# Query powers from a matmul on the decay table, a first loop period in its own order, a table cleared in steps

## The chip, the cores and the metric

The kernel runs on one core of a Trainium2 chip. The metric is the device time of one execution in microseconds (us), and less is better. TensorE (PE in the profile, PEld for its weight loads), VectorE (DVE), ScalarE (ACT), GpSimd (POOL) and SyncE (SP) each run their own instruction queue in order. DMA transfers are issued from SP, ACT and POOL; an engine whose next instruction has to wait holds up all that stands behind it in its queue.

## The reference

Two layers follow each other. The first is a causal linear attention with a decay per head, for 4 sequences of 768 positions, 8 heads of 64 channels, worked in blocks of positions:

```python
Dmask = np.where(rel >= 0, lam ** rel, 0.0)              # decay inside a block
lam_pow = lam ** (pos + 1)                               # query powers
intra = (q k^T * Dmask) v
inter = (q * lam_pow) @ kv_state
out = intra + inter
kv_state = lam ** block * kv_state + (k * lam ** (block - 1 - pos))^T v
```

The second is a mixture of experts on the 3072 tokens of 512 channels that come out: logits with a bias by modality, the best of 8 experts per token, `relu(x @ w1[e]) @ w2[e]`, scaled by the softmax weight of the chosen expert.

## The kernel before

All arithmetic that matters is float32 or its split into two parts. A sequence is cut into 6 blocks of 128 positions, and two blocks make a half, loaded by one `load_half` into a tile `load` of which there are three (`LOADS`). The attention runs over 12 periods of a pair of blocks. The first pair is written out ahead of the loop, the others are turns `j` of `for j in range(1, pairs)`. In a period TensorE makes the scores of both blocks (`scores`, L235), the part of the output that comes from the carried state (`from_state`, L281), the part from inside the block (`outputs`, L288), the token rows and gate logits of the pair before (`tokens`, L299), and the key-value products for the next states (`key_values`, L255). VectorE multiplies the scores by the decay table (`masked`, L242), the keys by their decay (`keys`, L213), the queries by their powers (`queries`, L225), and adds a faded state to a key-value product (`carried`, L270). GpSimd multiplies the old state by the decay of a block (L268). The tile `qd` of scaled queries has one buffer, so the queries of a pair can be scaled only when `from_state` of the pair before has read its own.

The tables are made on the chip. `spread_decays` spreads the 8 decays to all partitions with a tiny matmul and lets VectorE run one scan for each of the 8 heads, which gives `dk`, 128 columns for a head (L85). Four more scans give the query powers `pq` (L91), after two copies that arrange the decays by pair of heads (L89).

The mixture part needs a table `inv` in DRAM that maps slots to tokens. It is first filled with a padding value by four transfers (`clear_table`, L177), and then each block's tokens are scattered into it by an indirect DMA that GpSimd issues (`write_slots`, L392). A sequence's six scatters are spread over the period after its routing is known; the first sequence's begin in turn 5 of the loop. Each scatter writes to a place known only at run time, so it waits for all four clearing transfers.

The order on an engine is fixed in three ways: `pinned` chains the instructions of an engine in the order in which they are written; `behind(a, b)` adds an edge, a real wait or, with `wait=False`, an order alone; and what is left free is placed by a planner that goes by its own estimate of when things are ready. The fades are pinned on GpSimd, the scatters are not: they are held behind the fades written before them and behind the matmul named in the code. SP's queue is the order of the loads: in turn `j` it issues half `3 + j`, when its buffer is free, and the four clearing transfers stand behind half 5, in turn 2.

After the attention, tiles of 256 tokens of one expert go through the two layers of that expert, with weights fetched for each tile.

Of the kernel before, what the change touches and what calls it, by code (L numbers as in the profile page):

```python
# [6 lines left out]
F32 = mybir.dt.float32  # L7
# [4 lines left out]
ALU = mybir.AluOpType  # L12
# [28 lines left out]
def linear_attention_moe(tc, qkv, lam, modality, wg, mbias, w1, w2, out):  # L41
    nc = tc.nc
    with ExitStack() as ctx:
# [32 lines left out]
        lamp = const.tile([P, NP], F32, name="lamp")  # L76

        def spread_decays():

            lp = ps.tile([P, 2, NP], F32, name="x", bufs=1)  # L80
            pinned(nc.tensor.matmul(lp.rearrange("p h a -> p (h a)"), row, lam1, start=True, stop=True))
            pinned(nc.vector.tensor_copy(out=lamb, in_=lp))
            for hl in range(2):
                for p in range(NP):
                    pinned(nc.vector.tensor_tensor_scan(  # L85
                        out=dk[:, hl, p, :], data0=lamb[:, hl, p : p + 1].to_broadcast([P, P]),
                        data1=anti, initial=0.0, op0=ALU.mult, op1=ALU.add))
            for hl, r in enumerate(halves2):
                pinned(nc.vector.tensor_copy(out=lamp[r], in_=lamb[r, hl]))  # L89
            for p in range(NP):  # L90
                powers.append(pinned(nc.vector.tensor_tensor_scan(  # L91
                    out=pq[:, p, :], data0=lamp[:, p : p + 1].to_broadcast([P, P]),
                    data1=zero, initial=1.0, op0=ALU.mult, op1=ALU.add)))

        def load_tile():

# [11 lines left out]
        zero = const.tile([P, P], F32, name="zero")  # L108
        nc.vector.memset(zero, 0.0)
        anti = const.tile([P, P], F32, name="anti")  # L110
        nc.gpsimd.affine_select(out=anti, in_=zero, pattern=[[1, P]], compare_op=ALU.not_equal,
                                fill=1.0, base=1 - P, channel_multiplier=1)
        dk = const.tile([P, 2, NP, P], F32, name="dk")
        pq = const.tile([P, NP, P], F32, name="pq")
        powers = []
        ident = const.tile([P, P], F32, name="ident")
        make_identity(nc, ident)

        wgt = const.tile([P, HB, NP, E], F32, name="wgt")

        def later(op):

            behind(op, powers[-1])
            return op


        iw = const.tile([P, HB, NP, P + E], F32, name="iw")
# [20 lines left out]
                                          in_=ident[r, r].unsqueeze(1).to_broadcast([D, NP, D]))  # L148

        def routing_constants():  # L150
            nc.vector.memset(onesb, 1.0)
            later(nc.gpsimd.affine_select(out=lowb, in_=onesb, pattern=[[1, P]], compare_op=ALU.is_gt,
                                          fill=0.0, base=0, channel_multiplier=-1))
            later(nc.gpsimd.iota(desc, pattern=[[-1, E]], base=E, channel_multiplier=0,
                                 allow_small_or_imprecise_dtypes=True))
            later(nc.gpsimd.memset(pay, 0))
            nc.gpsimd.iota(pay[:, :, 0:1], pattern=[[P, B * NC]], base=0, channel_multiplier=1)

            for m in range(2):
# [12 lines left out]
        def clear_table(ld):  # L172
            for i in range(2):
                part = inv[i * half_inv : (i + 1) * half_inv, :].rearrange("(p r) c -> p r c", p=P)
                for r in range(0, half_inv // P, some):
                    dst = part[:, r : min(r + some, half_inv // P)]
                    behind(nc.sync.dma_start(out=dst, in_=pad[:, : dst.shape[1]]), ld, wait=False)  # L177

        state = [const.tile([P, NP, D], F32, name=f"state{i}") for i in range(3)]
        kdec = const.tile([P, HB, NP, 2], F32, name="kdec")  # L180
# [4 lines left out]
        def load_half(g):  # L185
            t = load_tile()
            whole = slice(0, HB)
            for part in (slice(0, 2), slice(2, 4)) if g < LOADS else (slice(0, 4),):
                for c in (slice(i, i + 1) for i in range(HB)) if g == 1 else (whole,):
                    ld = nc.sync.dma_start(out=t[:, part, c], in_=source(g)[:, part, c])  # L190
                    if g == 1 and part.start == c.start == 0:
                        nc.sync.dma_start(out=wgt, in_=wg)
            loads.append(ld)
            return t

# [42 lines left out]
        def masked(g, sp):  # L238

            pt = work.tile([P, 2, NP, P], F32, name="pt", bufs=2)  # L240
            for hl in (slice(0, 1), slice(1, 2)) if g == 0 else (slice(0, 2),):
                pinned(nc.vector.tensor_tensor(out=pt[:, hl], in0=sp[:, hl], in1=dk[:, hl], op=ALU.mult))  # L242
            return pt

        def key_values(gs):
# [29 lines left out]
        def from_state(j, op, qd):  # L275

            c = HB * j % NC
            for p in range(NP):
                for blk in range(0 if c else 1, HB):
# [570 lines left out]
                halves[j] = load_half(j)  # L850

        identities()
        c0, c1 = slice(0, 1), slice(1, 2)
        list_constants()
        keep_busy(4)
        spread_decays()
        keep_busy(8)
        sps = [scores(0)]
        keep_busy(2)
        sps.append(scores(1))  # L860
        keep_busy(4)
        for blk in range(HB):
            pinned(nc.scalar.copy(out=kdec[:, blk], in_=dk[:, :, :, P - 1].rearrange("p h a -> p a h")))
        more(1)
        more(2)
        for to, src in ((mod, modality), (mb, mbias.partition_broadcast(P))):
            behind(nc.sync.dma_start(out=to, in_=src), loads[-1], wait=False)
        pts = [masked(0, sps[0])]
        kds[0] = keys(0, c0)
        pts.append(masked(1, sps[1]))  # L870
        qds[0] = queries(0, c1, eng=nc.gpsimd)
        op = outputs_begin()
        kp, _ = key_values([0])
# [1 line left out]
        xts[0], _ = outputs(0, pts[0], op)  # L875
        from_state(0, op, qds.pop(0))
        xts[1], _ = outputs(1, pts[1], op)
        keys(0, c1, kds[0])
        kp, _ = key_values([1])
        carried(1, kp)  # L880
        pinned(nc.scalar.copy(out=iw[:, :, :, P:], in_=wgt))
        more(LOADS)
        for j in range(1, pairs):
            turns = turned(j - 1)
# [2 lines left out]
            if routed is not None:  # L887
                rk = ranks(*routed)
            if j == 1:
                qds[1] = queries(1, c0)  # L890
                pts = [masked(gs[0], sps[0])]
                kds[1] = keys(1, c0)
                pts.append(masked(gs[1], sps[1]))
                queries(1, c1, qds[1])
                next(turns)
                next(turns)
                kp, _ = key_values(gs[:1])
                carried(gs[0], kp)
                keys(1, c1, kds[1])
# [7 lines left out]
            if j == pairs - 1:  # L907
                halved = [pinned(nc.scalar.copy(out=w1h[i], in_=raw1[i])) for i in range(2)]
            op = outputs_begin()
            from_state(j, op, qds.pop(j))  # L910
            if j > 1:
                mm = next(turns)
            if j == early + 1:
                write_slot(mm)
# [21 lines left out]
            if j > 1:  # L936
                next(turns)
# [96 lines left out]
        kept = [dk[:, t].rearrange("p a t -> p (a t)") for t in range(2)]  # L1034

        def run_early(n):

# [102 lines left out]
```

## Time and profile before

| | |
|---|---|
| median of 3 runs | 413.11 us (413.05 to 416.46) |
| the profiled execution | 412.88 us, span 411.2 us |
| granted TensorE clock, mean | 0.992 |
| PE busy | 395.3 us, 96% |
| DVE busy | 252.4 us, 61% |
| ACT busy | 181.6 us, 44% |
| POOL busy | 113.6 us, 28% |
| moved by DMA | 63.28 MB |

The span runs from the first to the last instruction of the core; the time of the execution has 1.7 us more around it. All times in the rows below are microseconds from the start of the span. "PE busy" says that TensorE has something in flight, not that it runs at its peak.

### The profile page before, as it was taken

The numbers are of one execution on the slowest core, as the hardware profiler recorded it, in microseconds if no ns is written. First come the engines' busy times: TensorE is split into PE (matmuls) and PEld (weight loads), VectorE is DVE, ScalarE is ACT, GpSimd is POOL, SyncE is SP. The second block draws the span as 40 slices with busy tenths as digits, with TensorE's granted clock in tenths as the row PEclk, the third lists the DMA queues.
The fourth block names the chain that finished last, engine by engine and source line by source line (L and its number), as shares of the span: only waits on it lengthen the run. The fifth ranks groups of instructions, "written<-read, shape, count | busy, mean of one in ns | idle before, by whom it ended". The sixth has DMA issues, their size and how long they took to land.

```text
span 411.2 us, 9569 instructions
## 1 busy us (share of the span) xinstructions
PE 395.3 (96%) x3839; PEld 354.5 (86%) x3840; DVE 252.4 (61%) x438; ACT 181.6 (44%) x274; POOL 113.6 (28%) x119
## 2 busy tenths in 40 slices
PE   8899999999999999999999999999999999999990
PEld 4799999888998987898989898998989899998970
DVE  8776886967989813583665738374664828374510
ACT  1233233225655514473654638273555637264510
POOL 6301143352376510321130402222030312202000
PEclk9999999999999999999999999999999999999996
DMA  7999999994910292211063676211020211100000
GB/s 288 392 363 373 389 348 348 338 390 133 330 41 30 51 396 106 64 40 68 1 213 125 233 255 220 92 30 58 22 80 27 56 51 47 51 2 28 27 29 20
DMA packets 22677, 63.28 MB, mean 154 GB/s; under 512 B 6751, under 2 KB 7263, under 8 KB 20578
## 3 DMA queue, kind: packets, MB, share of 16 engines
q1 hardware_dynamic: 14400, 42.83, 29.1%
q0 software_dynamic: 4768, 13.08, 9.6%
q10 hardware_dynamic: 3458, 6.69, 4.3%
q8 instruction: 32, 0.52, 0.5%
q14 instruction: 19, 0.16, 0.1%
HBM read 90.87 MB, written 14.07 MB: 255 GB/s over the span
## 4 chain that ended last, share of the span: by engine, by line
PE 61%; issue 21%; DMA 7%; POOL 5%; DVE 3%; another core or an unknown queue 1%; ACT 1%; POOLq 1%; DVEq 0%; ACTq 0%
DMA out_dram<-y,idx 7%; PE s L639 6%; PE s L642 6%; PE s L643 6%; PE o L288 5%; PE o L639 5%; PE o L643 5%; PE o L642 5%; PE x L299 5%; PE s L235 5%; PE o L281 3%; POOL out_dram L715 3%; PE kv L255 2%; POOL xg L591 2%; PE s L674 1%
## 5 line engine op out<-in xcount | busy, mean ns | idle before, releaser
L639 PE MATMUL s<-xh,w1h 128*128 128x256 f32 x384 | 108.9, 284 | 0.8 <-DVE hl L657 0.8
L642 PE MATMUL s<-xl,w1h 128*128 128x256 f32 x384 | 108.4, 282 | 0.0
L643 PE MATMUL s<-xh,w1l 128*128 128x256 f32 x384 | 107.9, 281 | 0.0
L657 DVE SCALAR_TENSOR_TENSOR hl<-s,hh 128x512 fp32r<-128x512 f32 x48 | 33.1, 690 | 83.9 <-ACT hh L656 83.2
L639 PE MATMUL o<-w2h,hh 128*128 128x512 f32 x192 | 75.9, 395 | 0.0
L643 PE MATMUL o<-w2h,hl 128*128 128x512 f32 x192 | 74.8, 390 | 0.0
L642 PE MATMUL o<-w2l,hh 128*128 128x512 f32 x192 | 74.8, 389 | 0.0
L639 PEld LDWEIGHTS s<-xh,w1h 128*128 128x128 f32 x384 | 72.0, 187 | 1.9 <-DVE hl L657 1.0
L643 PEld LDWEIGHTS s<-xh,w1l 128*128 128x128 f32 x384 | 72.8, 190 | 0.0
L642 PEld LDWEIGHTS s<-xl,w1h 128*128 128x128 f32 x384 | 72.2, 188 | 0.4
L556 DVE TENSOR_TENSOR w2l<-raw,w2h 128x1024 fp32r<-128x1024 f32 x48 | 58.8, 1225 | 11.0 <-ACT w2h L555 10.5
L656 ACT ACTIVATE hh<-s 128x512 fp32r<-128x512 f32 x48 | 28.7, 598 | 71.0 <-PE s L643 67.3
L556 DVE TENSOR_TENSOR w1l<-raw,w1h 128x1024 fp32r<-128x1024 f32 x46 | 53.5, 1217 | 4.9 <-ACT yn L703 3.4
L555 ACT CAST w2h<-raw 128x1024 fp32r<-128x1024 f32 x48 | 49.9, 1040 | 0.0
L591 POOL DMA_INDIRECT xg<-xs,idx x20 | 24.0, 1202 | 87.0 <-PE kv L626 82.8
L715 POOL DMA_INDIRECT out_dram<-y,idx x18 | 26.2, 1457 | 78.1 <-ACT y L731 74.7
L555 ACT CAST w1h<-raw 128x1024 fp32r<-128x1024 f32 x46 | 45.2, 1063 | 0.4 <-issue 0.4
L643 PEld LDWEIGHTS o<-w2h,hl 128*128 128x128 f32 x192 | 36.0, 188 | 7.6
L642 PEld LDWEIGHTS o<-w2l,hh 128*128 128x128 f32 x192 | 36.1, 188 | 7.1
L639 PEld LDWEIGHTS o<-w2h,hh 128*128 128x128 f32 x192 | 36.1, 188 | 7.1
L301 ACT COPY xn<-x 128x272 f32<-128x272 f32 x42 | 16.3, 388 | 46.1 <-PE x L299 43.0
L392 POOL DMA_INDIRECT inv<-pay,sloti x24 | 28.5, 1189 | 22.3 <-PE x L299 8.1
(215 smaller groups left out, 468.3 us busy)
## 6 DMA issues: line engine op xcount, KB each, us to landing
raw<-in_w_dram SPq DMA_DIRECT2D x52, 1024.0 KB
load<-in_qkv_dram SPq DMA_DIRECT2D x9, 2048.0 KB
xs<-xn ACTq DMA_DIRECT2D x24, 272.0 KB
load<-in_qkv_dram SPq DMA_DIRECT2D x8, 512.0 KB
load<-in_qkv_dram SPq DMA_DIRECT2D x2, 1024.0 KB
w2f<-in_w_dram SPq DMA_DIRECT2D x2, 1024.0 KB
w1h<-in_w_dram SPq DMA_DIRECT2D x2, 1024.0 KB
inv<-pad SPq DMA_DIRECT2D x2, 196.0 KB
```

Source lines behind the costliest of these rows:

```text
L235: pinned(nc.tensor.matmul(sp[:, hl, p, :], kt[r, p, :], qt[r, p, :], start=True, stop=True))
L288: mm = pinned(nc.tensor.matmul(op[blk][halves2[hl ^ blk], p, :], vt[:, (2 * p + hl) * D : (2 * p + hl + 1) * D], pt[:, hl, p, :], start=(g ...
L392: sc = nc.gpsimd.indirect_dma_start(out=inv, out_offset=bass.IndirectOffsetOnAxis(ap=at, axis=0), in_=pay[:, c, :], in_offset=None)
L555: cp = nc.scalar.copy(out=hi, in_=src)
L556: df = nc.vector.tensor_tensor(out=lo, in0=src, in1=hi.bitcast(F32), op=ALU.subtract)
L591: last = nc.gpsimd.indirect_dma_start(out=(to or xg)[t][:m], out_offset=None, in_=xs[:rows, :], in_offset=bass.IndirectOffsetOnAxis(ap=idx ...
L639: mm = pinned(nc.tensor.matmul(out, ah, bh, start=first, stop=False))
L642: pinned(nc.tensor.matmul(out, ah, bl, start=False, stop=False))
L643: return pinned(nc.tensor.matmul(out, al, bh, start=False, stop=last))
L656: act = nc.scalar.activation(out=hh[i], in_=hp, func=AF.Relu)
L657: low = nc.vector.scalar_tensor_tensor(out=hl[i], in0=hp, scalar=0.0, in1=hh[i].bitcast(F32), op0=ALU.max, op1=ALU.subtract)
L715: sc = nc.gpsimd.indirect_dma_start(out=out, out_offset=bass.IndirectOffsetOnAxis(ap=idx[:, t, 0:1], axis=0), in_=y, in_offset=None, bound ...
```

## The change

- `dk` gets 129 columns for a head instead of 128 (so do `zero` and `anti`), so that its last row holds the powers 1 to 128 of the decay. The two copies and four scans on VectorE that made `pq` are gone. `spread_powers` multiplies a selector `last` (only its last row is one) with columns 1 to 128 of `dk`, two matmuls into one PSUM tile, and ScalarE copies that tile to `pq`. The masks read `dk` in rows of 129.
- Ahead of the loop, the fillers `keep_busy(2)` and `keep_busy(4)` go; `spread_powers` stands between the scores of block 0 and block 1; the copies to `kdec` come before it. The second keys of the first half come earlier on VectorE. The first half of the next pair's queries goes to GpSimd.
- In turn 1 the state of the first block is used ahead of the first token group, and the second block's after its own state is made; the token groups stand between other work.
- `clear_table` is a generator: one clearing transfer in turn 2, one in turn 3, two in turn 4, each behind the load issued just before it.
- `wgt`, `mod` and `mb`, three small inputs, are loaded from GpSimd's queue instead of SP's. The routing constants that GpSimd makes (`lowb`, `desc`, `pay`, `pad`), and the loads of `mod` and `mb`, are ordered behind the second fade and no longer behind the last scan.
- Half 2 comes in three pieces, keys by rows first, values last; half 3 comes in two.

```diff
-            for hl, r in enumerate(halves2):
-                pinned(nc.vector.tensor_copy(out=lamp[r], in_=lamb[r, hl]))
-            for p in range(NP):
-                powers.append(pinned(nc.vector.tensor_tensor_scan(
-                    out=pq[:, p, :], data0=lamp[:, p : p + 1].to_broadcast([P, P]),
-                    data1=zero, initial=1.0, op0=ALU.mult, op1=ALU.add)))
+        def spread_powers():
+            pp = ps.tile([P, NP, P], F32, name="x", bufs=1)
+            for hl, r in enumerate(halves2):
+                pinned(nc.tensor.matmul(pp[r], last, dk[:, hl, :, 1:], start=True, stop=True))
+            pinned(nc.scalar.copy(out=pq, in_=pp))
...
-        dk = const.tile([P, 2, NP, P], F32, name="dk")
+        dk = const.tile([P, 2, NP, P + 1], F32, name="dk")
...
+        last = const.tile([P, D], F32, name="last")
+        nc.gpsimd.affine_select(out=last, in_=zero[:, :D], pattern=[[0, D]], compare_op=ALU.not_equal,
+                                fill=1.0, base=1 - P, channel_multiplier=1)
...
+        nc.gpsimd.dma_start(out=wgt, in_=wg)
         def later(op):
-            behind(op, powers[-1])
+            behind(op, fades[1], wait=False)
...
         def routing_constants():
+            for to, src in ((mod, modality), (mb, mbias.partition_broadcast(P))):
+                later(nc.gpsimd.dma_start(out=to, in_=src))
...
-                    behind(nc.sync.dma_start(out=dst, in_=pad[:, : dst.shape[1]]), ld, wait=False)
+                    yield behind(nc.sync.dma_start(out=dst, in_=pad[:, : dst.shape[1]]), ld[-1], wait=False)
...
-            for part in (slice(0, 2), slice(2, 4)) if g < LOADS else (slice(0, 4),):
+            keyed, valued = (slice(0, 2), slice(2, 4)), (slice(3, 4), slice(0, 2), slice(2, 3))
+            for part in keyed if g in (1, LOADS) else valued if g < LOADS else (slice(0, 4),):
...
         keep_busy(8)
         sps = [scores(0)]
-        keep_busy(2)
+        spread_powers()
         sps.append(scores(1))
-        keep_busy(4)
...
-        keys(0, c1, kds[0])
+        pinned(nc.scalar.copy(out=iw[:, :, :, P:], in_=wgt))
+        qds[1] = queries(1, c0, eng=nc.gpsimd)
         kp, _ = key_values([1])
         carried(1, kp)
...
             if j == 1:
-                qds[1] = queries(1, c0)
+                queries(1, c1, qds[1])
                 pts = [masked(gs[0], sps[0])]
                 kds[1] = keys(1, c0)
                 pts.append(masked(gs[1], sps[1]))
...
             op = outputs_begin()
-            from_state(j, op, qds.pop(j))
-            if j > 1:
+            if j == 1:
+                from_state(1, op, qds[1], range(1))
+                next(turns)
+                kp, _ = key_values(gs[:1])
+                carried(gs[0], kp)
+                keys(1, c1, kds[1])
+            else:
+                from_state(j, op, qds.pop(j))
                 mm = next(turns)
...
+            if j == 1:
+                from_state(1, op, qds.pop(1), range(1, HB))
...
-            if j == 2:
-                clear_table(loads[-1])
+            if 2 <= j <= per + 1:
+                for _ in range(2 if j == per + 1 else 1):
+                    next(clearing)
```

## Rows read from the trace of the kernel before

**Rows 1.** The page, busy time by engine: busy us, share, instructions.

```profile
PE 395.3 (96%) x3839; PEld 354.5 (86%) x3840; DVE 252.4 (61%) x438; ACT 181.6 (44%) x274; POOL 113.6 (28%) x119
```

**Rows 2.** Busy time by stretch: stretch, us, engines (count), clock, DMA share, GB/s.

```profile
0.00:8.00 8.00, 6.59 (x34) 3.04 (x36) 6.07 (x27) 1.59 (x3) 5.55 (x21) 1.00 0.72 260
8.00:55.00 47.00, 45.13 (x872) 40.86 (x873) 35.68 (x66) 14.13 (x34) 10.11 (x15) 1.00 1.01 382
55.00:63.00 8.00, 8.00 (x150) 7.38 (x146) 5.29 (x6) 2.52 (x6) 4.52 (x5) 1.00 0.96 330
```

**Rows 3.** The chain that ended last, start of the span: start, us, what.

```profile
4.13 2.94 DVE dk L85 x8
...
7.34 1.01 DVE pq L91 x3
...
10.67 0.69 PE kv L255 x16
...
17.02 0.68 DVE kd L213
...
24.67 1.99 PE s L235 x32
...
32.18 1.99 PE s L235 x32
```

**Rows 4.** The timeline: start, us, engine, line, operation, tiles, [idle before].

```profile
8.80 1.27 POOL L225 TENSOR_TENSOR qd<-load,pq 128x512 f32<-128x512 f32 x1 [2.27 <-DVE pq L91]
11.19 1.05 PE L288 MATMUL o<-pt,load 128*64 128x128 f32 x16
11.67 0.67 DVE L213 TENSOR_TENSOR kd<-load,kdec 128x512 f32<-128x512 f32 x1
11.86 0.97 POOL L268 TENSOR_TENSOR faded<-state,pq 128x256 f32<-128x256 f32 x1 [0.29 <-ACT state L266]
24.85 0.62 POOL L268 TENSOR_TENSOR faded<-state,pq 128x256 f32<-128x256 f32 x1 [4.00 <-DVE state L270]
41.01 2.35 DVE L242 TENSOR_TENSOR pt<-s,dk 128x1024 f32<-128x1024 f32 x2
```

**Rows 5.** The timeline of SP's queue: when a transfer was issued.

```profile
9.63 0.34 SPq L867 DMA_DIRECT2D mod<-in_modality_dram  x1
...
31.04 2.96 SPq L177 DMA_DIRECT2D inv<-pad  x4
...
46.68 0.39 SPq L190 DMA_DIRECT2D load<-in_qkv_dram  x1
```

**Rows 6.** DMA issues by line: count and KB of each.

```profile
load<-in_qkv_dram SPq DMA_DIRECT2D x9, 2048.0 KB
xs<-xn ACTq DMA_DIRECT2D x24, 272.0 KB
...
inv<-pad SPq DMA_DIRECT2D x2, 196.0 KB
```

**Rows 7.** ACT's timeline: first and last of nine token stores issued before 55 us.

```profile
18.97 0.36 ACTq L303 DMA_DIRECT2D xs<-xn  x1
...
53.29 0.33 ACTq L303 DMA_DIRECT2D xs<-xn  x1
```

**Rows 8.** POOL's timeline around the first scatters, of which five precede 63.85.

```profile
53.63 1.27 POOL L392 DMA_INDIRECT inv<-pay,sloti  x1 [5.28 <-PE x L299]
55.20 0.96 POOL L392 DMA_INDIRECT inv<-pay,sloti  x1 [0.30 <-PE kv L255]
56.17 0.64 POOL L268 TENSOR_TENSOR faded<-state,pq 128x256 f32<-128x256 f32 x1
...
61.77 0.96 POOL L392 DMA_INDIRECT inv<-pay,sloti  x1 [0.68 <-PE x L299]
63.85 0.61 POOL L268 TENSOR_TENSOR faded<-state,pq 128x256 f32<-128x256 f32 x1 [1.12 <-DVE state L270]
```

**Rows 9.** The chain that ended last, turn 7: start, us, what.

```profile
65.12 1.03 PE o L281 x32
```

More of the change, by code (lines that the diff above doesn't have):

```diff
@@ L85, in spread_decays @@
                     pinned(nc.vector.tensor_tensor_scan(
-                        out=dk[:, hl, p, :], data0=lamb[:, hl, p : p + 1].to_broadcast([P, P]),
+                        out=dk[:, hl, p, :], data0=lamb[:, hl, p : p + 1].to_broadcast([P, P + 1]),
                         data1=anti, initial=0.0, op0=ALU.mult, op1=ALU.add))
+        def spread_powers():
+            pp = ps.tile([P, NP, P], F32, name="x", bufs=1)
             for hl, r in enumerate(halves2):
-                pinned(nc.vector.tensor_copy(out=lamp[r], in_=lamb[r, hl]))
-            for p in range(NP):
-                powers.append(pinned(nc.vector.tensor_tensor_scan(
-                    out=pq[:, p, :], data0=lamp[:, p : p + 1].to_broadcast([P, P]),
-                    data1=zero, initial=1.0, op0=ALU.mult, op1=ALU.add)))
+                pinned(nc.tensor.matmul(pp[r], last, dk[:, hl, :, 1:], start=True, stop=True))
+            pinned(nc.scalar.copy(out=pq, in_=pp))
         def load_tile():
@@ L107, in linear_attention_moe @@
         nc.vector.memset(busy, 0.0)
-        zero = const.tile([P, P], F32, name="zero")
+        zero = const.tile([P, P + 1], F32, name="zero")
         nc.vector.memset(zero, 0.0)
-        anti = const.tile([P, P], F32, name="anti")
-        nc.gpsimd.affine_select(out=anti, in_=zero, pattern=[[1, P]], compare_op=ALU.not_equal,
+        anti = const.tile([P, P + 1], F32, name="anti")
+        nc.gpsimd.affine_select(out=anti, in_=zero, pattern=[[1, P + 1]], compare_op=ALU.not_equal,
                                 fill=1.0, base=1 - P, channel_multiplier=1)
-        dk = const.tile([P, 2, NP, P], F32, name="dk")
+        dk = const.tile([P, 2, NP, P + 1], F32, name="dk")
         pq = const.tile([P, NP, P], F32, name="pq")
-        powers = []
+        last = const.tile([P, D], F32, name="last")
+        nc.gpsimd.affine_select(out=last, in_=zero[:, :D], pattern=[[0, D]], compare_op=ALU.not_equal,
+                                fill=1.0, base=1 - P, channel_multiplier=1)
         ident = const.tile([P, P], F32, name="ident")
@@ L187, in load_half @@
             whole = slice(0, HB)
-            for part in (slice(0, 2), slice(2, 4)) if g < LOADS else (slice(0, 4),):
+            keyed, valued = (slice(0, 2), slice(2, 4)), (slice(3, 4), slice(0, 2), slice(2, 3))
+            for part in keyed if g in (1, LOADS) else valued if g < LOADS else (slice(0, 4),):
                 for c in (slice(i, i + 1) for i in range(HB)) if g == 1 else (whole,):
                     ld = nc.sync.dma_start(out=t[:, part, c], in_=source(g)[:, part, c])
-                    if g == 1 and part.start == c.start == 0:
-                        nc.sync.dma_start(out=wgt, in_=wg)
             loads.append(ld)
@@ L241, in masked @@
             for hl in (slice(0, 1), slice(1, 2)) if g == 0 else (slice(0, 2),):
-                pinned(nc.vector.tensor_tensor(out=pt[:, hl], in0=sp[:, hl], in1=dk[:, hl], op=ALU.mult))
+                pinned(nc.vector.tensor_tensor(out=pt[:, hl], in0=sp[:, hl], in1=dk[:, hl, :, :P], op=ALU.mult))
             return pt
@@ L273, in outputs_begin, with from_state @@
             return [ps.tile([P, NP, P], F32, name="o", bufs=2) for _ in range(HB)]
-        def from_state(j, op, qd):
+        def from_state(j, op, qd, blks=range(HB)):
             c = HB * j % NC
             for p in range(NP):
-                for blk in range(0 if c else 1, HB):
+                for blk in blks if c else blks[1:]:
                     for hl, r in enumerate(halves2):
@@ L852, in linear_attention_moe @@
         identities()
+        clearing = clear_table(loads)
         c0, c1 = slice(0, 1), slice(1, 2)
@@ L856, in linear_attention_moe @@
         spread_decays()
+        for blk in range(HB):
+            pinned(nc.scalar.copy(out=kdec[:, blk], in_=dk[:, :, :, P - 1].rearrange("p h a -> p a h")))
         keep_busy(8)
         sps = [scores(0)]
-        keep_busy(2)
+        spread_powers()
         sps.append(scores(1))
-        keep_busy(4)
-        for blk in range(HB):
-            pinned(nc.scalar.copy(out=kdec[:, blk], in_=dk[:, :, :, P - 1].rearrange("p h a -> p a h")))
         more(1)
         more(2)
-        for to, src in ((mod, modality), (mb, mbias.partition_broadcast(P))):
-            behind(nc.sync.dma_start(out=to, in_=src), loads[-1], wait=False)
         pts = [masked(0, sps[0])]
@@ L870, in linear_attention_moe @@
         pts.append(masked(1, sps[1]))
+        keys(0, c1, kds[0])
         qds[0] = queries(0, c1, eng=nc.gpsimd)
@@ L877, in linear_attention_moe @@
         xts[1], _ = outputs(1, pts[1], op)
-        keys(0, c1, kds[0])
+        pinned(nc.scalar.copy(out=iw[:, :, :, P:], in_=wgt))
+        qds[1] = queries(1, c0, eng=nc.gpsimd)
         kp, _ = key_values([1])
         carried(1, kp)
-        pinned(nc.scalar.copy(out=iw[:, :, :, P:], in_=wgt))
         more(LOADS)
@@ L893, in linear_attention_moe @@
                 pts.append(masked(gs[1], sps[1]))
[L894 to L899, printed above, removed]
             else:
@@ L935, in linear_attention_moe @@
             write_slot(mm)
-            if j > 1:
-                next(turns)
+            next(turns)
             kp, _ = key_values((gs[1], gs[1] + 1))
@@ L1032, in run @@
             return second(idx, turned, kept if n == fixed_ones - 1 else None)
-        kept = [dk[:, t].rearrange("p a t -> p (a t)") for t in range(2)]
+        kept = [dk.rearrange("p h a t -> p (h a t)")[:, t * DM : (t + 1) * DM] for t in range(2)]
         def run_early(n):
```

1 line of the change is left out of this document (removed).

## The prediction

> **What bounds the kernel now.** I read the page first. TensorE is busy 96% of the span [rows 1], so time can come only out of the waits of its queue. The change touches the first 25 us and the table that the experts' part reads, so I went next to the chain of waits at the start of the span. Ahead of the first key-value product at 10.67 it is VectorE's: eight scans until 7.07, four more until 8.35, masks and keys [rows 3]. From 24.67 on it is TensorE's, and a period there takes 7.51 us (24.67 to 32.18) [rows 3]. The period ahead of it, the loop's first, begins after the key-values of the first pair at about 14.7 and so takes 9.9.
>
> The third view is the busy time by stretch. The DMA engines are full from 8 us on: share 1.01 until 55 us at 382 GB/s, 0.96 after it at 330 [rows 2]. So a transfer lands when all that was queued ahead of it on SP has been moved; issuing it earlier does not help much. The reader is to see that two engines are near their limit in the attention, and that the change moves work on both.
>
> **The start.** The copies and four scans hold the chain from 7.07 to 8.35, 1.28 us [rows 3]. In their place stand two matmuls of 512 columns, on TensorE, ahead of the scores of block 1. Nothing in the trace has their shape. Eight matmuls with the same contraction and output rows, also 1024 columns in all, took 1.05 us [rows 4]; if the two halves of the output do not overlap as those do, twice that, 2.1. I take 1.3, nearer to the first, since output rows alternate in both. From 7.07 that gives 8.4, and with one block's scores (half of 1.99 us [rows 3]) and a few hand-overs the first key-values start at 9.7 instead of 10.67: 1.0 us gained (0.2 to 1.3). A scan of 129 columns instead of 128 adds under 1% of 2.94 us. The fillers that go had no reader. The copy to `pq` is ScalarE's, idle then, and the GpSimd queries, which started at 8.80 [rows 4], start about half a us later, still ahead of their reader.
>
> **The first period.** GpSimd now scales block 2's queries too (1.27 us [rows 4]). That must wait for `from_state` of block 1 because `qd` has one buffer, and the first fade stands behind it. From 9.7, key-values (0.7), a block of outputs (0.9) and `from_state` (1.0) give 12.3 for the first; then 13.6 for the end of the queries, 14.3 for the fade at 0.62. VectorE then adds the state (0.4), scales one block of queries, masks one and scales one block of keys (0.7, 1.2, 0.7): these keys end at about 17.35, where they ended at 17.70 [rows 3]. So the head of the period gains only 0.35. Its tail gains more: after these keys TensorE has 7.51 less 1.99 of scores, less half a `from_state` (0.5) and one token group (0.5), plus one block's key-values (0.5), so 5.0 us without a wait, against 6.97 until 24.67. Scores of the next pair come at 22.4: 2.2 us earlier, which I round to 2.1 (0.4 to 2.6).
>
> Fades took 0.97 us at 11.86 and 0.62 at 24.85; at 11.86 VectorE had keys in work from 11.67 to 12.34 [rows 4]. I take 0.62, since VectorE waits for this fade and does nothing else; at 0.97 the gain would be 0.35 us less.
>
> The Trainium skill (SBUF — State Buffer, Who interferes with whom) says that a VectorE instruction with two SBUF inputs and a GpSimd instruction that reads SBUF lock each other out, and it speaks against scaling queries on GpSimd. The trace agrees: 12.34 plus half a us is where the slow fade ended. By that rule the fade is free of it here, and 2.1 us stands; without it I would take the mean of both rows and 1.9.
>
> **Small inputs.** No plain load on GpSimd's queue is in the trace. The nearest rows are the scatters, 0.96 to 1.27 us [rows 8]; a price near zero is the other end. Three loads then take up to 3.8 us. One falls ahead of 8.80, where GpSimd idled 2.27 us [rows 4]; two fall with the routing constants behind the second fade, and next in that queue is the third, which the state needs only at the end of the period. They are hidden; without that cover the price would be about 1 us in the first period. On SP three issues of about 0.4 us go and three pieces are added, in a queue that waits for buffers anyway. The new order of half 2 changes only what lands first of it.
>
> **The table.** Here I expect the gain to go. Six scatters of the first sequence begin at 53.63 [rows 8], and each waits for all four clearing transfers. Those were issued at 31.04 [rows 5], behind half 5. Now the last two stand behind half 7, issued at 46.68 [rows 5] and some 2 us earlier after the change. When do they land? The stretches give 2.08 MB by 8 us and 20.03 MB by 55 [rows 2]. First the delay from moved to landed: half 0 (2.10 MB) is moved at 8.0, and the load of `mod` on SP, which waits for it, goes at 9.63 [rows 5]: 1.6 us. Ahead of the end of the last clear stand eight halves (16.78 MB), 0.79 MB of clears, 0.07 of small inputs, and nine token stores of 0.28 MB [rows 6, 7]: 20.15 MB, which at 330 GB/s is moved at 55.4 and landed at 57.0. With eight stores it is 56.2, with ten and a delay longer by half a us 58.3.
>
> GpSimd's queue stands still until then, where its first scatter could have gone at about 51.6. Behind the first scatter stand, in the order of the trace, a second, a fade, three more scatters, and the fade of 63.85 [rows 8]. At 1.27 for the first, 0.97 for the others, 0.64 for the fade and 0.3 between scatters they take 7.0 us, so that fade starts at 64.0. Before, it started at 63.85 after 1.12 us of idling [rows 8], and `from_state` of turn 7 followed 1.27 later, at 65.12, as part of the chain [rows 9]: no slack. So turn 7 starts its state part 0.15 us later than before, whatever was gained earlier. Next late is TensorE itself, busy from there on. Later sequences' scatters meet a cleared table.
>
> The sum of this case: the profiled execution took 412.88, and 412.88 + 0.15 = 413.0; the median of the runs shown lies 0.23 above it, so **413.3**. With landing from 56.2 to 58.3 and scatters of 0.96 to 1.27, it is 412.4 to 414.6.
>
> The Trainium skill (DMA: Bandwidth & Descriptors, Queues, rings and completion order) has transfers of one issuing engine consumed in ring order, with the completion count written after all earlier writes of that DMA engine; by that the clears cannot land before half 7. No row before shows a clear right behind a load with a reader waiting.
>
> **Rivals.**
> A. The forecast above: first-loop gain returned at the scatters. For it: the full DMA engines and the fade without slack. Against it: the margin is small, the whole gain lies between landings at 54.9 and at 57.0. Chance 0.55.
> B. The gain stays. The planner can place the fades ahead of the scatters, since the scatters are not pinned and it goes by its own estimate; or the clears land by 54.9, from where 7.0 us of GpSimd work ends in time for a turn 7 earlier by 2.1 us. Then 412.88 − 2.1 + 0.23 = 411.0 (410.5 to 412.7). The first fade of rows 8 was placed ahead of a scatter that stands before it in the code, which shows that this can be. Chance 0.3.
> C. A part of it: some scatters behind the fade, 412. Chance 0.1. Here too belongs that clearing in steps frees nothing for the loads, which were not late after the first period.
> D. Slower: the masks read `dk` in rows of 129 elements. Two of them take 2.35 us a period [rows 4], and VectorE is busy 35.7 of 47 us [rows 2], so 1.8 us of a period are free. If the step cost a factor of two, a period would grow by 2.35 − 1.8 = 0.55 us, and eleven of them by 6: 419. It decides from a factor of 1.8. Against it: keys, with an operand broadcast along its rows, take 0.67 us for 512 elements [rows 4], as much for an element as the masks with none (1.18 us for 1024). Chance 0.03.
>
> **How the numbers follow.** About 1% is what a measurement of this kernel can tell from no change, 4.1 us. A, B and C all lie within it: 0.94 for no change. Faster by more needs over 4.1 us, more than the 1.0 us of scans and all waiting of the first period together: 0.02 for what I have overlooked. Slower has D and a landing after 61 us: 0.04. The range takes B's likeliest value and A's upper bound, 410.9 to 414.6. A's own is 412.4 to 414.6.
>
> **What would show it.** The key-values of block 0 near 9.7; no scan at L91; scores of the second loop period near 22.4. For A: the first scatter ends an idle time of GpSimd of several us that a clear ends, near 57, the fade of turn 7 starts near 64, and TensorE waits ahead of `from_state` of turn 7 for VectorE's state. For B: the same fade near 62 and no such wait. It is wrong if the clears land well before 55 or if the scores of turn 2 stay at 24.7. Masks longer than 1.2 us each would be D.

## The result and the profile after

The changed kernel takes 417.25 us in the median (414.35 to 419.45, 20 runs) against 413.15 (412.47 to 416.46, 20 runs): ratio 1.0093 [1.0075, 1.0111], slower by 3.8 us. The forecast was 413.3, with 410.9 to 414.6 as its range. The profiled execution took 415.5 us (span 413.8), so it is one of the quicker; a second profile, of 418.2 us, comes below under E5. The kernel before takes 410.4 to 413.2 us on the chips used here, so experiments are read by their ratio to it on their own chip.

The page of the changed kernel: busy time by engine, and the clock that was granted to TensorE in 40 slices of the span.

```profile
PE 397.3 (96%) x3838; PEld 356.0 (86%) x3838; DVE 250.9 (61%) x431; ACT 182.2 (44%) x275; POOL 117.2 (28%) x124
...
PEclk9999998999999999999999999999999999999997
```

The shares are those of before [rows 1]. The news is in the clock's row: slice 7, from 62 to 72 us, has an 8 where the kernel before had a 9:

```profile
PEclk9999999999999999999999999999999999999996
```

The next views say what stands on either side of it. First the start, in the chain that ended last (start, us, what).

```profile
3.81 2.48 PE o L819 x8
...
7.39 1.01 PE x L92 x4
...
9.49 0.61 PE kv L259 x16
...
22.82 1.99 PE s L239 x32
30.32 1.99 PE s L239 x32
```

Against [rows 3]: the first key-values come at 9.49 instead of 10.67, the scores of the second loop period at 22.82 instead of 24.67, and the period behind them is 7.50 us as before. So 1.85 us are gained, and TensorE's chain stands where VectorE's stood. That gain lasts until the scores at 53.49 (55.34 before). The timeline of GpSimd and VectorE in the first period:

```profile
9.14 1.32 POOL L229 TENSOR_TENSOR qd<-load,pq 128x512 f32<-128x512 f32 x1 [1.29 <-ACT pq L93]
...
12.15 1.27 POOL L229 TENSOR_TENSOR qd<-load,pq 128x512 f32<-128x512 f32 x1 [1.69 <-PE o L285]
13.38 0.62 POOL L272 TENSOR_TENSOR faded<-state,pq 128x256 f32<-128x256 f32 x1
...
14.37 0.68 DVE L229 TENSOR_TENSOR qd<-load,pq 128x512 f32<-128x512 f32 x1
14.53 1.00 POOL L272 TENSOR_TENSOR faded<-state,pq 128x256 f32<-128x256 f32 x1 [0.53 <-DVE state L274]
...
15.48 0.63 POOL L155 DMA_DIRECT2D mod<-in_modality_dram  x1
16.10 0.54 POOL L155 DMA_DIRECT2D mb<-in_mbias_dram  x1
16.11 0.68 DVE L217 TENSOR_TENSOR kd<-load,kdec 128x512 f32<-128x512 f32 x1
```

Then the table. SyncE's queue (half 7, and right behind it the last two clears):

```profile
44.83 0.37 SPq L196 DMA_DIRECT2D load<-in_qkv_dram  x1
45.24 1.18 SPq L182 DMA_DIRECT2D inv<-pad  x2
```

GpSimd's timeline, the first scatter and the two fades behind it; five scatters stand ahead of the second:

```profile
59.08 1.13 POOL L396 DMA_INDIRECT inv<-pay,sloti  x1 [12.58 <-PE x L303]
...
61.50 0.64 POOL L272 TENSOR_TENSOR faded<-state,pq 128x256 f32<-128x256 f32 x1
...
65.86 0.63 POOL L272 TENSOR_TENSOR faded<-state,pq 128x256 f32<-128x256 f32 x1
```

And the chain through turn 7:

```profile
66.53 0.43 DVE state L274
...
67.00 1.97 PE o L285 x28
...
74.15 1.87 PE s L239 x29
```

GpSimd stands still for 12.58 us ahead of its first scatter (5.28 before [rows 8]) and the fade of turn 7 starts at 65.86 instead of 63.85. TensorE, which was ready at 64.5, idles for 2.53 us; `from_state` of turn 7 starts at 67.00 instead of 65.12 [rows 9]. The idle time is put down to "PE x L303", one of the several things that the scatter waits for. E1 shows that it was the clears.

The last view shows what the chain does not: stretches of 1 us (busy time of PE, PEld, DVE, ACT, POOL; then the granted clock, the DMA share, GB/s).

```profile
66.00:67.00 1.00, 0.00 (x0) 0.00 (x0) 0.47 (x2) 0.00 (x0) 0.83 (x2) 0.77 0.92 346
67.00:68.00 1.00, 0.99 (x20) 1.00 (x24) 1.00 (x1) 0.00 (x0) 0.97 (x2) 0.50 0.99 376
...
69.00:70.00 1.00, 1.00 (x10) 1.00 (x12) 1.00 (x3) 0.00 (x0) 0.00 (x0) 0.52 1.00 400
70.00:71.00 1.00, 1.00 (x22) 1.00 (x20) 1.00 (x2) 0.39 (x1) 0.00 (x0) 1.00 0.23 80
```

Behind the idle time the granted clock is 0.50, the 1.2 GHz level, until 70. From `from_state` to the next scores it takes 7.15 us (67.00 to 74.15), against 5.72 before (65.12 [rows 9] to 70.84): 1.43 us more. So of this execution's +2.6 us, 1.88 are the late start of turn 7, 1.43 the clock, and some 0.7 are made up again until the end.

### The profile page after: what moved, and what is told of

It reads as the page before. It is cut to its first block, busy times and chain, and to the rows that moved or that the text cites. A ratio compares the mean times of both kernels' runs of the same rounds, so it can differ in the third digit from the quotient of the medians.

```text
span 413.8 us, 9571 instructions
## 1 busy us (share of the span) xinstructions
PE 397.3 (96%) x3838; PEld 356.0 (86%) x3838; DVE 250.9 (61%) x431; ACT 182.2 (44%) x275; POOL 117.2 (28%) x124
## 4 chain that ended last, share of the span: by engine, by line
PE 45%; issue 34%; POOL 8%; DMA 6%; ACT 2%; DVE 2%; another core or an unknown queue 1%; POOLq 1%; SPq 1%; DVEq 0%; ACTq 0%
PE o L292 5%; PE x L303 5%; PE s L239 5%; POOL out_dram L719 4%; PE s L643 3%; PE s L647 3%; PE s L646 3%; PE o L285 3%; DMA idx<-inv 3%; PE o L643 3%; PE o L647 3%; PE o L646 3%; POOL xg L595 2%; PE kv L259 2%; DMA xg<-xs,idx 2%
## 5 line engine op out<-in xcount | busy, mean ns | idle before, releaser
L719 POOL DMA_INDIRECT out_dram<-y,idx x18 | 27.5, 1529 | 76.7 <-ACT y L735 76.7
```

The costliest lines, as they stand in the source:

```text
L719: sc = nc.gpsimd.indirect_dma_start(out=out, out_offset=bass.IndirectOffsetOnAxis(ap=idx[:, t, 0:1], axis=0), in_=y, in_offset=None, bound ...
```

## The experiments

**E1 and E2: the clears early again.** Theory 1: the late clears hold GpSimd's queue, that makes the state of turn 7 late, and TensorE loses the time there. Its rival: something else of the change is slow (the loads in pieces, full DMA engines). E1 puts the two last clears ahead of half 7 in turn 4; E2 puts all four into turn 2. Their edits, in this order:

```diff
-            more(LOADS + j)
-            if 2 <= j <= per + 1:
-                for _ in range(2 if j == per + 1 else 1):
+            if j == per + 1:
+                for _ in range(2):
                     next(clearing)
+            more(LOADS + j)
+            if 2 <= j <= per:
+                next(clearing)
```
```diff
-            if 2 <= j <= per + 1:
-                for _ in range(2 if j == per + 1 else 1):
+            if j == 2:
+                for _ in range(4):
```

> The changed kernel with one edit: in turn 4 the two last clearing transfers are issued ahead of half 7 instead of behind it. Theory 1 (the last clears land late, GpSimd's queue stands still behind the first scatter, the state of turn 7 is late): they land near 51 instead of 58.6, the first scatter goes when its matmul is done, near 52, TensorE does not wait ahead of the state part of turn 7, and the 1.85 us gained at the start stay: 411.3 us. Theory 2 (TensorE runs ahead of the loads and the DMA engines, which moved 251 to 294 GB/s between 62 and 82 us, are the loss): the bytes are the same, 416 to 418.

> The changed kernel with all four clears in turn 2 again, behind half 5. Theory 1: 411.3 us, the first scatter near 52. Theory 2: as changed or worse, since 0.8 MB stand ahead of half 6 again: 416 to 419. If the small inputs on GpSimd's queue or the rows of 129 cost time, it shows here too, above 411.3.

E1: ratio 0.9967 [0.9953, 0.9982] (the brackets hold the 95% interval). E2: 0.9964 [0.9947, 0.9980]. All of the loss goes, and a gain of 1.4 us stays. E1's GpSimd:

```profile
52.90 1.18 POOL L396 DMA_INDIRECT inv<-pay,sloti  x1 [5.24 <-PE x L303]
...
62.54 0.63 POOL L272 TENSOR_TENSOR faded<-state,pq 128x256 f32<-128x256 f32 x1
```

Only the place of two transfers in SyncE's queue differs, and the wait falls from 12.58 to 5.24 us: the clears were what the scatter waited for. No idle time stands ahead of turn 7. But E1's chain at the start is not that of the change:

```profile
3.81 3.52 PE o L819 x8
...
10.65 0.61 PE kv L259 x16
...
23.98 1.99 PE s L239 x32
...
94.35 1.99 PE s L239 x32
```

The eight fillers (`keep_busy`, matmuls of zeros that nobody reads) took 3.52 us instead of 2.48 and now stand on the path, so only 0.69 of the 1.85 us were gained by the second loop period (E7, E8 and E10 take this up).

**E3: the kernel before with its clears in steps and nothing else of the change.**

```diff
-                    behind(nc.sync.dma_start(out=dst, in_=pad[:, : dst.shape[1]]), ld, wait=False)
+                    yield behind(nc.sync.dma_start(out=dst, in_=pad[:, : dst.shape[1]]), ld[-1], wait=False)
...
-            if j == 2:
-                clear_table(loads[-1])
+            if 2 <= j <= per + 1:
+                for _ in range(2 if j == per + 1 else 1):
+                    next(clearing)
```

> The kernel before with one edit: the clears in steps (one in turn 2, one in turn 3, two in turn 4). Theory 1: the last clear lands as in the changed kernel, near 58.6, so the fade of turn 7 starts near 66 and the state part near 67 where it was 65.1; with 2.0 us of idle TensorE and about 1.4 us at the lower clock after it the loss is 3.4 us or more: 416.5 to 418. Theory 2: no change, 413.1.

Ratio 1.0157 [1.0135, 1.0179]: this part alone makes more than the whole loss. The five runs are 412.88, 416.71, 416.80, 417.16 and 417.90, with mean clocks of 0.993 and four times 0.985. The profile is of the first; `from_state` of turn 7 waits there as in the change, but the granted clock stays at its high level:

```profile
68.14 1.09 PE L281 MATMUL o<-qd,state 64*64 64x128 f32 x28 [2.45 <-DVE state L270]
```

**E4: the change, clears late as they are, the first sequence's scatters held to turn 7** (one, one and four, behind that turn's fades).

```diff
-            if slots and slots[0][0] < SOON * NC:
-                write_slots([slots.pop(0)], after)
-                behind(written[-1], fades[-1], wait=False)
+            for _ in range(many):
+                if turn > 2 * per and slots and slots[0][0] < SOON * NC:
+                    write_slots([slots.pop(0)], after)
+                    behind(written[-1], fades[-1], wait=False)
...
-            write_slot(mm)
+            write_slot(mm, 4 if j == 2 * per + 1 else 1)
```

> The changed kernel, clears as late as there, but the first sequence's six scatters are all held until turn 7, so that no fade of turns 5 and 6 stands behind one in GpSimd's queue. Theory 1, its second half (it is the fades behind the waiting scatter that cost, not the late clears as such): 411.3 to 412, no idle TensorE ahead of the state part of turn 7. If the late clears cost in another way (the loads behind them on SP's queue), 416 to 418.

Ratio 0.9982 [0.9960, 1.0003]. The clears are as late as in the change, yet nothing waits: a late clear costs only what stands behind the waiting scatter in GpSimd's queue. Its timeline:

```profile
62.70 0.62 POOL L272 TENSOR_TENSOR faded<-state,pq 128x256 f32<-128x256 f32 x1 [0.53 <-DVE state L274]
66.21 1.38 POOL L396 DMA_INDIRECT inv<-pay,sloti  x1 [2.88 <-PE o L292]
```

**E5 to E8** ran on one chip. E5 is the change once more. E6 fills its idle time:

```diff
             else:
+                if j == 2 * per + 1:
+                    keep_busy(14, "x", 1)
                 from_state(j, op, qds.pop(j))
```

> The change itself once more, with nothing altered, as the yardstick of this chip. Theory (the late clears hold GpSimd's queue, the state of turn 7 is late, TensorE idles 2.5 us ahead of its from_state and its granted clock then falls to the 1.2 GHz level for some us): ratio 1.008 to 1.011 to the kernel before, the runs spread over some 5 us because the clock falls in some of them and not in others; in the profile of a run near the median the rows of 1 us behind 66 show the low level for longer than the 3.7 us of the first profile, 5 to 8 us. Rival (the clock plays no part, the loss is the idle time and the work behind it alone): the same ratio, but a run near the median has no more us at the low level than the first profile, and the surplus lies elsewhere.

E5: 1.0086 [1.0055, 1.0117], runs from 414.47 (clock 0.993) to 418.83 (0.985). Its profile is of a usual run, 418.2 us. `from_state` of turn 7, and two of the stretches of 1 us behind it:

```profile
67.60 1.97 PE L285 MATMUL o<-qd,state 64*64 64x128 f32 x28 [3.35 <-DVE state L274]
```

```profile
67.00:68.00 1.00, 0.40 (x8) 0.40 (x12) 0.88 (x2) 0.00 (x0) 0.83 (x2) 0.50 1.03 413
...
72.00:73.00 1.00, 1.00 (x12) 1.00 (x10) 0.86 (x5) 0.57 (x1) 0.00 (x0) 0.50 0.00 0
```

The low level lasts until 73.4, so 5.8 us of work instead of 3. The next scores come at 76.14, 8.54 us behind `from_state`: 2.82 us more than before's 5.72, twice the first profile's 1.43. With a start of turn 7 that is 2.48 us late this makes 5.3 at 76.14 and 5.0 at the end of the span.

> The change with 14 matmuls of 512 columns (zeros, result unused) on TensorE right ahead of from_state in turn 7, where it otherwise idles for 2.5 us; the clears stay late, so the state comes as late as before. 14 x 0.213 us = 3.0 us at the high level, so from_state starts 0 to 0.5 us later than in the change. Theory of the clock: the granted clock stays at 1.00 behind them, the 1.4 us (quick run) to about 4 us (usual run) of the low level go away: ratio 1.002 to 1.006, spread of the runs under 3 us. Rival (idle time alone counts, the clock does not): 1.008 to 1.012, no quicker than the change.

E6: 1.0083 [1.0048, 1.0118]. By its time the rival is right, though the interval reaches into both ranges. The clocks are 0.990 to 0.992 in every run, and in the profile `from_state` to the next scores take 5.77 us (68.74 to 74.51), so the low level is gone; but the state came later:

```profile
64.82 3.19 PE L819 MATMUL x<-busy 128*128 128x512 bf16 x14
67.95 0.44 PE L285 MATMUL o<-qd,state 64*64 64x128 f32 x4
68.74 1.09 PE L285 MATMUL o<-qd,state 64*64 64x128 f32 x28 [0.35 <-DVE state L274]
```

In this execution the eight fillers of the start took 3.52 us, the loop and with it the clears' issue ran 1.3 to 1.5 us behind E5, and the first scatter started at 60.17. The two effects could not be told apart here; E9 was made for that.

E7 has the clears in turn 2 and five fillers at the start; E8 has the clears in turn 2, eight fillers and the powers by VectorE's scans. Both edits stand on top of E2's:

```diff
-        keep_busy(8)
+        keep_busy(5)
```
```diff
-            pp = ps.tile([P, NP, P], F32, name="x", bufs=1)
             for hl, r in enumerate(halves2):
-                pinned(nc.tensor.matmul(pp[r], last, dk[:, hl, :, 1:], start=True, stop=True))
-            pinned(nc.scalar.copy(out=pq, in_=pp))
+                pinned(nc.vector.tensor_copy(out=lamp[r], in_=lamb[r, hl]))
+            for p in range(NP):
+                pinned(nc.vector.tensor_tensor_scan(
+                    out=pq[:, p, :], data0=lamp[:, p : p + 1].to_broadcast([P, P]),
+                    data1=zero[:, :P], initial=1.0, op0=ALU.mult, op1=ALU.add))
...
         spread_decays()
+        spread_powers()
```

> The change with its four clears issued in turn 2 (as in the kernel before's place for their landing, in good time for the scatters) and with 5 instead of 8 matmuls of zeros ahead of the first scores. Theory (behind the repaired clears the gain of the start is cut because those eight matmuls, 3.5 us where TensorE still runs at the low level, now stand on the path to the first key-values): five of them take at most 2.15 us, the first scores start by 6.3 and the first key-values by 9.6 in every run: 0.9 us less than with eight where the clock rose late, nothing where it rose early; ratio 0.994 to 0.996 (0.9964 with eight). Rival (the load of the first tile or the table of decays holds the first scores anyway): same as with eight, 0.9964, the wait named as a DMA or VectorE. A second rival: fewer matmuls let the clock rise later, and the first period gets slower by up to 1 us: 0.997 to 0.999.

E7: 0.9960 [0.9939, 0.9980], no better than E1 and E2. The start is as quick as expected in its chain:

```profile
3.81 2.20 PE o L819 x5
...
9.48 0.61 PE kv L259 x16
...
22.81 1.99 PE s L239 x32
```

But the scores that E1 has at 94.35 come at 94.51: the lead of 1.17 us over E1 at the second loop period is lost again by then. On the way TensorE waits 0.40 and 0.59 us ahead of `tokens` at 77.14 and 84.29, as it did before the change at 78.56 and 85.71 (0.43 and 0.63); E1 waits once in that stretch, 0.50 us ahead of `from_state` at 80.56. What sets these waits was not followed further.

> The change with its four clears issued in turn 2, and with the query powers by the two copies and four scans on VectorE of the kernel before instead of TensorE's two matmuls: it keeps the changed order of the first period, the small inputs and eight matmuls of zeros. Splits the gain of the start. Theory (as forecast, the powers by TensorE are worth about 1.0 us of the first key-values and the order of the first period about 1.1 us more): first key-values at 10.7, scores of the next pair at 23.7 to 24.0, ratio 0.997 to 0.999, i.e. 0.2 to 1 us slower than with the matmuls. Rival (the powers' matmuls win nothing, since with them the eight matmuls of zeros are the path): first key-values as with matmuls at 10.4 to 10.7, ratio 0.9955 to 0.9970.

E8: 0.9995 [0.9974, 1.0016], above what either theory expected. First TensorE's timeline, then the chain:

```profile
10.96 0.69 PE L262 MATMUL kv<-load,kd 128*64 128x64 f32 x16 [1.76 <-DVE kd L220]
```

```profile
10.96 0.69 PE kv L262 x16
...
24.36 1.99 PE s L242 x32
```

TensorE waits for VectorE ahead of the first key-values, so here the eight fillers are off the path, and E7 with its five can be set beside it. With the scans the second loop period starts at 24.36: 0.31 us ahead of the kernel before, 1.55 behind E7. The powers by TensorE are worth 1.55 of the 1.86 us (and 0.9995 to 0.9960, 1.4 us, in the time); the order of the period is worth the small rest. From the first key-values to these scores it takes 13.40 us, against 14.00 before [rows 3] and 13.33 in E7, so the order wins 0.6 us there, of which 0.29 are lost ahead of the key-values (10.96 for 10.67). I had powers and order about even.

**E9: E3 with its idle time filled by 12 matmuls.** There the start cannot blur it, since its fillers lie beside VectorE's scans.

```diff
+            if j == 2 * per + 1:
+                keep_busy(12, "x", 1)
             from_state(j, op, qds.pop(j))
```

> The kernel before with its clears in steps, as in the change, and nothing else of the change (1.0157 without what follows), and with 12 matmuls of zeros on TensorE ahead of from_state in turn 7, where it idled for 2.45 us: 12 x 0.213 = 2.6 us. The start cannot blur it here, since its matmuls of zeros lie beside VectorE's scans. Theory of the clock (the idle time costs some 3 us as a late state and then some 1.4 to 3 us more at the 1.2 GHz level): the granted clock is .990 or more in every run, the usual run is about as long as the quick run of the kernel without them (412.88 against 410.36), ratio 1.005 to 1.010. Rival (the late state alone makes the loss and its spread, the clock follows from it and costs nothing): ratio 1.013 to 1.018.

E9: 1.0081 [1.0061, 1.0102] against E3's 1.0157 [1.0135, 1.0179], clocks 0.990 to 0.993 in all runs. Its profile, of the longest run:

```profile
66.09 2.76 PE L815 MATMUL x<-busy 128*128 128x512 bf16 x11
68.79 0.44 PE L281 MATMUL o<-qd,state 64*64 64x128 f32 x4
70.64 1.09 PE L281 MATMUL o<-qd,state 64*64 64x128 f32 x28 [1.42 <-DVE state L270]
```

(One of the twelve has no record.) Twelve matmuls whose result nobody reads take 0.0076 of the time, 3.1 us, off E3's 6.4 us of loss, each kernel against the one before on its own chip, although the state came as late as 70.6 in this run. The clock stays at its high level in E9's profile. So about half of what late clears cost there is the clock, the other half the wait.

**E10 to E12.** E10 is the change with five fillers at the start; E11 adds the 12 ahead of turn 7; E12 is E7 with the small inputs on SyncE's queue again (`wgt` in `load_half`, `mod` and `mb` behind half 2):

```diff
-        nc.gpsimd.dma_start(out=wgt, in_=wg)
+                    if g == 1 and part.start == c.start == 0:
+                        nc.sync.dma_start(out=wgt, in_=wg)
-                later(nc.gpsimd.dma_start(out=to, in_=src))
+            behind(nc.sync.dma_start(out=to, in_=src), loads[-1], wait=False)
```

> The change with five instead of eight matmuls of zeros ahead of the first scores, its clears late as they are: yardstick for the next kernel. Theory: the start is the quick one in every run (first key-values at 9.5), the loss in turn 7 is unchanged: ratio 1.006 to 1.010, clocks from .982 to .993. Rival (an early start makes the clears and their scatters early too, so that the loss shrinks by as much): 1.003 to 1.006.

E10: 1.0066 [1.0043, 1.0089]. Its start was not the quick one in the profiled run:

```profile
5.99 2.08 PE L239 MATMUL s<-load 64*128 64x128 f32 x16
8.00 1.97 PE L92 MATMUL x<-dk,last 128*64 128x512 f32 x4
```

Scores that take 1.16 us elsewhere and powers that take 1.08 need twice the time here: with fewer fillers, the matmuls behind them are the slow ones. This is the second rival of E7, seen here.

> The change with five matmuls of zeros ahead of the first scores and 12 ahead of from_state in turn 7 (2.6 us, less than the 2.5 to 3.4 us of idle time there). Theory of the clock: granted clock 1.00 in the rows of 1 us behind 66, from_state at 67 to 68, 5.8 us from there to the next scores (8.5 at the low level); clocks .990 or more in every run, ratio 1.001 to 1.006, and 0.003 to 0.006 below the kernel with five alone. Rival (the low level costs nothing that the late state does not cost anyway): as with five alone, within 0.002.

E11: 1.0087 [1.0060, 1.0114], no quicker than E10, so the expectation failed. The fillers ended at 66.45, and the state came so late in this run that the idle time stood behind them again; the clock fell in the stretches behind it:

```profile
68.96 1.09 PE L285 MATMUL o<-qd,state 64*64 64x128 f32 x28 [2.52 <-DVE state L274]
```

```profile
71.00:72.00 1.00, 1.00 (x14) 0.50 0.03 9
```

E11's six runs fall in two groups: three with a mean clock of 0.990 to 0.993 take 413.1 to 413.8 us, three with 0.987 or 0.988 take 415.4 to 415.9. That fits a price of the clock, but a later state in the second group would bring both, so it does not show it.

> The change with its clears in turn 2, five matmuls of zeros, and the three small inputs (router weights, modality, bias) loaded from SyncE's queue as in the kernel before instead of GpSimd's. Tells what that part of the change is worth. Theory (hidden either way, as forecast): 0.996 as with GpSimd's queue, within 0.001. Rival (the router weights ahead of the second tile's pieces in SyncE's queue put the second scores or the second pair's keys off): 0.997 to 0.999, a DMA wait in the first 25 us.

E12: 0.9964 [0.9950, 0.9978], as E7 and E2. The small inputs are worth nothing measurable in either queue. E1, E2, E7 and E12 are the versions that beat both kernels, the one before by 0.3 to 0.4% with intervals below 1.

## Why the prediction was wrong

**The step that failed is the table's sum**, in two of its terms: the time at which the last clear has landed, and the last link, "Next late is TensorE itself, busy from there on". The mechanism is the one forecast as A: GpSimd's queue stands still behind the first scatter until the clears land, the gain of the first loop is given back at turn 7, TensorE waits there for VectorE's state. E1, E2 and E4 confirm each link. Two things made 417 out of 413.3.

The first is a size. I had the last clear moved at 55.4 and landed at 57.0 (56.2 to 58.3), with the first scatter there; it started at 59.08 in the first profile and at 59.72 to 62.66 in E3, E5, E6 and E9 to E11. The 1.6 us from moved to the waiting reader held: by the trace's DMA records the scatter started 1.43 to 1.57 us behind the end of the last clear's last packet in all seven. The error is when that packet is moved: at 57.59 in the first profile, at 58.29 to 61.14 in the others. Ten token stores, not nine, were issued ahead of 55 us, 0.28 MB or 0.8 us. The mean rate was not the error: the stretches of 8 to 55 and 55 to 63 us moved 382 and 362 GB/s, against 382 and 330 in [rows 2]. The rest, 1.4 us, is that the sum goes by the mean rate while a transfer ends with its last packet: of the last clear's 128 packets half had ended by 54.6 and nine tenths by 56.9 in the first profile, nine tenths by 55.4 and the last at 58.29 in E5. Why the last ones come so late, and by how much in which execution, stays open. The sum behind the scatter was right: 7.0 us forecast, 6.78 measured (59.08 to 65.86). So the start of turn 7 became 1.88 us late instead of 0.15, in the first profile, and 2.48 in E5.

The second is a term that is missing. I let TensorE's idle time cost its own length. It costs more: in the work behind it the granted clock is 0.50, for 1.43 us in the first profile, 2.82 in E5, and 3.1 us by E9 against E3. In the change itself no run with the wait filled was quicker beyond noise (E6, E11), so there the price rests on the two profiles. The kernel before gave no sign of it: its granted clock is 1.00 in every stretch of [rows 2], because it has no such wait. A forecast with such a wait in it needed this as a rival on the slow side; mine, D, sat elsewhere.

**The start was right** in its sum, and in parts by luck. Powers: 1.3 us forecast, 1.01 in the chain, near the bound of 1.05; key-values 9.49 for 9.7. The scans that went had held the chain for longer than I read: the row that ends at 8.35 [rows 3] holds three of the four, and the masks behind them began at 8.63. Scores of the second loop period: 22.82 for 22.4, 1.85 us gained for 2.1. The keys of block 2 ended at 16.79 (16.11 + 0.68), not 17.35, but the stretch behind them took 6.03 us, not 5.0: two errors that cancel in part. And the path was another: the chain does not leave TensorE between 9.49 and 22.82, so these keys were not on it. What I missed is that the fillers, once VectorE's scans are gone, stand on the path, so that TensorE's slow first microseconds reach the loop: key-values at 9.5 to 11.1 over the profiles with TensorE's powers. That takes up to 1.6 us of the gain, though E7 shows that the time at the end hardly depends on it.

**The lock** held: the fade at 13.38, with VectorE idle, took 0.62 us, and the one at 14.53, beside VectorE's queries, 1.00. That agrees with the Trainium skill (SBUF — State Buffer, Who interferes with whom), by which a VectorE instruction with two SBUF inputs and a GpSimd instruction that reads SBUF lock each other out.

**Small inputs** were hidden, as forecast, at 0.54 to 0.71 us each instead of up to 1.27 (E12).

**The rivals.** B's price was right for its condition: with the clears landed in time, the ratio is 0.9960 to 0.9967, 1.4 to 1.7 us of 413, for 2.1 forecast. I gave it 0.3 and the planner did not bring it about; its order on GpSimd stayed that of before. D is refuted: 23 masks of 1024 elements average 1217 ns, 1215 before.

## What to carry to other kernels

When a transfer is moved back in a queue, look for the one instruction that waits for it, and then for what stands behind that instruction on its engine; here scatters that E4 could hold back for another 7 us at no measurable loss held up a state that TensorE needed at once. Price an idle time of the bounding engine with what follows it, not with its length. And when an engine's work leaves the path, ask what filler or warm-up beside it becomes the path.

## What the runs showed of the hardware

- TensorE's granted clock fell to 0.50 behind idle times of 2.53, 3.35, 3.52 and 2.52 us (the change, E5, E10, E11), but not behind 2.45 us in E3's profiled run, while four other runs of E3 have a mean clock of 0.985. E3's runs have two lengths, some 4 us apart; a mean clock lower by 0.008 over 415 us makes 3.3 us of that, by estimate. Where matmuls filled most of the wait (E6, E9), the profile shows no fall.
- At the start of the span matmuls take twice their later time (0.43 us for 512 columns), until 5 us in some executions and until 10 in E10, although the column of the granted clock reads 1.00 there. That 1.00 is no reading: the trace's record of the granted clock begins only at 5.1 us in the change, 7.6 in E1 and 10.0 in E10, about where the matmuls become quick. A kernel whose first matmuls are on its path inherits that difference.
- A wait for several things is put down to one of them: "PE x L303" stands in the profiles of the change and of E1, with 12.58 and 5.24 us, and a DMA was what ended the longer one.
